# An output product built from seven block products: transformer block, forward and backward, on one core

## The chip, the cores and the metric

The kernel runs on one core of one Trainium2 chip. The metric is the time of one execution on the device, in microseconds. The core has a matrix engine (TensorE, PE in the profile), a vector engine (VectorE, DVE), a scalar engine (ScalarE, ACT), a general engine (GpSimd, POOL) and a queue engine (SyncE, SP). Matmuls read SBUF and write PSUM, the accumulator memory; the other engines read PSUM back. DMA engines move data between SBUF and HBM; SP, POOL and ACT issue their transfers.

## What is computed

One transformer block with linear attention and a SwiGLU feed-forward part, and its gradients: 2048 tokens, width 640, 32 heads of 20, feed-forward width 1728, all in bfloat16. The seven outputs are the block's result and the gradients of x, wqkv, wo, w_gate, w_up and w_down.

```python
def _A_ref(x, wqkv, wo):                      # linear attention
    pq, pk = phi(q), phi(k)                   # q, k, v from x @ wqkv
    kv = einsum("bhsd,bhse->bhde", pk, v); z = einsum("bhsd->bhd", pk)
    o = einsum("bhqd,bhde->bhqe", pq, kv) / (einsum("bhqd,bhd->bhq", pq, z)[..., None] + 1e-6)
    return o.reshape(B, S, D) @ wo
def _B_ref(x, w_gate, w_up, w_down):
    return (silu(x @ w_gate) * (x @ w_up)) @ w_down

h  = x + _A_ref(layernorm(x), wqkv, wo)
h2 = h + _B_ref(layernorm(h), w_gate, w_up, w_down)
out, grads = h2, vjp(grad_out)                # of x, wqkv, wo, w_gate, w_up, w_down
```

The change lies in the last product, h2 = h + m @ w_down, with m = silu(gate) * up.

## The kernel before

Tokens are cut into 16 tiles of 128. The width 640 is 5 blocks of 128, and a result row of 640 is computed as two chunks of 320 columns, each in its own PSUM bank. The feed-forward width 1728 is 13 blocks of 128 and a last one of 64.

The stages, in order: first layer norm, keys and queries; attention forward through folded weights; second layer norm; for each of four column groups of the feed-forward width, gate and up products, the elementwise part, and the weight gradients (`dw_group`, where dW_gate and dW_up are already made by seven block products with sums on VectorE); the backward pass through the feed-forward part into dh1; the gradients of the attention part (dk, dx, dW_q, dW_k); and last the output product. m was stored to HBM (`scr_m`) in the feed-forward stage, and h (`scr_h1`) in the attention stage.

The stage before the change, line 1024 on, walks over the tiles. For each it forms dk (`ps_dk`) and, three tiles later, dx (`ps_dxn`, 30 matmuls) with a layer norm backward (`ln_bwd`, lines 141 to 152): ACT reads PSUM, VectorE multiplies, ACT again, VectorE adds twice, and POOL stores dx. `dwqk(1, i)` is part i of dW_k: 32 matmuls that accumulate over the 16 token tiles, twice for the two chunks, then a convert on ACT (line 991) and a store. Parts 0 to 2 lie between the last tiles, parts 3 and 4 behind them.

The output stage takes one token tile after another (`part`, line 1121). A tile of m, transposed on load by SP (`load_mT`, line 1022), is the stationary operand, w_down (`wd`) the moving one. The 13 full blocks need 13 matmuls a chunk. The last block has only 64 rows: its matmul takes half of the array's rows. w_down's last 64 rows are held twice, in the lower and in the upper partitions, so that the half matmuls of two chunks can stand side by side on the two halves of the array. They are collected: `halves_at` does those of tiles 0 to 3 in one block of eight behind tile 1, of 4 to 7 behind tile 5, and so on, five blocks in all. VectorE adds h (`h1r`, loaded by POOL) to the finished PSUM row (line 1128), and POOL or SP stores it. Between tiles, `small_of` places the six blocks of dW_o (two matmuls each, line 1082) and the five of dW_v (seven small ones, line 127), each with a convert on ACT and a store. The operands of dW_v come from `scr_Yt` by six transposes on SP.

PSUM is four tiles of two banks (`mm`); a new one waits until an earlier one has been read. SBUF pools work in the same way: `big` has five large slots, `strips` four. In the region around this stage SP and DVE issue in the order in which the code is written; PE, ACT and POOL are ordered by the scheduler.

Of the kernel before, what the change touches and what calls it, by code (L numbers as in the profile page):

```python
# [8 lines left out]
FP32 = mybir.dt.float32  # L9
BF16 = mybir.dt.bfloat16  # L10
ALU = mybir.AluOpType
ACT = mybir.ActivationFunctionType
AX = mybir.AxisListType
EngineType = mybir.EngineType

P = 128
# [4 lines left out]
def kernel(  # L21
# [8 lines left out]
    nc = tc.nc  # L30
    _, S, D = A_x.shape
    F = B_w_gate.shape[1]
    Dh = D // H
    ST = S // P
    DT = D // P
    NCH = [(0, 320), (320, 640)]
    LAG = 3
# [6 lines left out]
    FT = 14  # L44
    GM = 448
    MTA = 5
# [5 lines left out]
    o0_v = out_0.rearrange("b (t p) d -> p (b t) d", p=P)  # L52
# [5 lines left out]
    big = ctx.enter_context(tc.tile_pool(name="big", bufs=5))  # L58
# [3 lines left out]
    def mm(name):  # L62

        return psum.tile([P, 2, 512], FP32, name=name, tag="mm")

    def row(ps):
        return ps[:, :, :320]

    def half(ap):
        return ap.rearrange("p (c n) -> p c n", c=2)  # L70
# [3 lines left out]
    def wk(name, w=D, pool=0):  # L74
        return wpools[pool].tile([P, w], BF16, name=name, tag="w", padded_shape=[P, D])
# [13 lines left out]
    scr_Yt = dram.tile([D, D], BF16, name="scr_Yt")  # L89
# [22 lines left out]
    OH = [120 * j for j in range(5)] + [D - P]  # L112
    HC = [(0, 120)] * 5 + [(88, P)]
    HG = len(OH)
# [64 lines left out]
    def fw(name):  # L179
        return fpool.tile([P, 2, GM], BF16, name=name, tag="f")  # L180
# [297 lines left out]
    with tc.manual_schedule(engines={EngineType.PE, EngineType.DVE, EngineType.SP, EngineType.Pool}):  # L478
# [25 lines left out]
        for i in range(DT):  # L504
            ps = mm("ps_y")
            for ci, (n0, n1) in enumerate(NCH):
                for t in range(ST):
                    nc.tensor.matmul(ps[:, ci, :320], lhsT=xn[:, t, i * P:(i + 1) * P], rhs=pk[:, t, n0:n1],  # L508
                                     start=(t == 0), stop=(t == ST - 1))
# [55 lines left out]
        for t in range(ST + 2):  # L565
            if t < ST:
                xr = wk("h1")
                ps = mm("ps_a")
                for ci, (n0, n1) in enumerate(NCH):
                    for i in range(DT):  # L570
                        nc.tensor.matmul(ps[:, ci, :320], lhsT=pqsT[:, i, t * P:(t + 1) * P], rhs=W2[:, i, n0:n1],  # L571
                                         start=(i == 0), stop=(i == DT - 1))
# [12 lines left out]
            while h1_todo and h1_todo[0][0] < t:  # L585
                v, h1 = h1_todo.pop(0)
# [5 lines left out]
            u = t - 2  # L592
# [23 lines left out]
    with tc.manual_schedule(engines={EngineType.SP}):  # L616
# [105 lines left out]
        for g in range(4):  # L722
            w = GW[g]
# [3 lines left out]
            for t in range(0, ST, 2):  # L727
                pg = mm("pg")
                for c in range(2):
                    for kt in range(DT):  # L730
                        nc.tensor.matmul(pg[:, c, :w], lhsT=hnT[:, kt, (t + c) * P:(t + c + 1) * P], rhs=wg[:, kt, 0:w],  # L731
                                         start=(kt == 0), stop=(kt == DT - 1))
                pu = mm("pu")
                for c in range(2):
                    for kt in range(DT):
                        nc.tensor.matmul(pu[:, c, :w], lhsT=hnT[:, kt, (t + c) * P:(t + c + 1) * P],  # L736
                                         rhs=wg[:, kt, w:2 * w], start=(kt == 0), stop=(kt == DT - 1))
                ddt = dd[t // 8]
                tt = t % 8
# [10 lines left out]
                u = fw("u")[:, :, :w]  # L750
# [88 lines left out]
    def mat(at, k, w):  # L839
        return mats[:, at:at + k * w].rearrange("p (k w) -> p k w", k=k)  # L840
# [5 lines left out]
    with tc.manual_schedule(engines={EngineType.SP, EngineType.Pool}):  # L846
# [20 lines left out]
        for t in range(ST + LAG_C):  # L867
# [14 lines left out]
            u = t - LAG_C + 1  # L882
# [15 lines left out]
            u = t - LAG_C  # L898
# [14 lines left out]
            S1 = small.tile([P, H], FP32, name="S1", tag="S1", bufs=3)  # L913
# [9 lines left out]
    with tc.manual_schedule(engines={EngineType.SP, EngineType.DVE}):  # L923
# [13 lines left out]
        def tr_cols(dst, src, c):  # L937
            nc.sync.dma_start_transpose(out=dst.unsqueeze(1), in_=src[:, c:c + P])
# [24 lines left out]
        Y = mat(2 * HG * P + HG * D, HG, D)  # L963
# [7 lines left out]
        def load_pqT(v):  # L971
            nc.sync.dma_start_transpose(out=ring[:, 4 + v % 3], in_=scr_pk[v * P:(v + 1) * P, :])
            nc.sync.dma_start_transpose(out=ring[:, 7 + v % 3], in_=dq[v // 8][:, v % 8, :])
# [4 lines left out]
            nc.scalar.copy(out=half(WK2[:, i, :]), in_=row(ps))  # L978
            nc.sync.dma_start_transpose(out=WV2[:, :, i * P:(i + 1) * P], in_=WK2[:, i, :])

        def dwqk(which, i, between=None):
            ev = wk("dwqk", pool=i % 2)
            ps = mm("ps_dwqk")
            for ci, (n0, n1) in enumerate(NCH):
                for t in range(ST):
                    nc.tensor.matmul(ps[:, ci, :320], lhsT=xn_r[:, t, i * P:(i + 1) * P],  # L986
                                     rhs=dq[t // 8][:, t % 8, n0:n1] if which == 0 else dk[:, t, n0:n1],
                                     start=(t == 0), stop=(t == ST - 1))
                if between and ci == 0:
                    between()  # L990
            nc.scalar.copy(out=half(ev[:]), in_=row(ps))
            nc.gpsimd.dma_start(out=out_2[i * P:(i + 1) * P, which * D:(which + 1) * D], in_=ev[:])

        load_pqT(0)
        for t in range(ST):
# [3 lines left out]
        for t in range(ZL, ZL + 2):  # L999
            dz_add(t, ztmp)  # L1000
        dwqk(0, 0)
        kv_blocks(dKVT, "ps_dkvt", lambda i, a, b: woT[:, i, a:b], lambda i, a, b: GT[:, i, a:b])
        for t in range(ZL + 2, ST):
            dz_add(t, ztmp)
        dzs = [wk("dzs"), wk("dzl")]
        nc.vector.tensor_copy(out=dzs[0][:], in_=zacc[:])
        nc.vector.tensor_tensor(out=dzs[1][:], in0=zacc[:], in1=dzs[0][:], op=ALU.subtract)
        dwqk(0, 1)
        for i in range(3):
            wk2(i)  # L1010
# [6 lines left out]
        mTs = {}  # L1017

        def load_mT(t):
            if t % 4 == 0:  # L1020
                mTs[t // 4] = strips.tile([P, 4, FT, P], BF16, name="mT", tag="S")
            nc.sync.dma_start_transpose(out=mTs[t // 4][:, t % 4], in_=scr_m[t * P:(t + 1) * P, :])

        for t in range(ST + LAG):
            if t in (2, 3):
                dwqk(0, t + 1)
            if t < ST:
                if t + 2 < ST:
# [7 lines left out]
                                               in1=half(dzb[:]), op0=ALU.mult, op1=ALU.add)  # L1036
# [11 lines left out]
            if t == ST:  # L1048
                wd = big.tile([P, FT, D], BF16, name="wd", tag="B")
# [3 lines left out]
            u = t - LAG  # L1053
# [6 lines left out]
            for ci, (n0, n1) in enumerate(NCH):  # L1060
                for k, (lhs, rhs) in enumerate(((dqT, wqkvT[:, 0:5]), (pkT, WV2), (dkT, wqkvT[:, 5:10]))):
                    for i in range(DT):
                        nc.tensor.matmul(ps[:, ci, :320], lhsT=lhs[:, i, :], rhs=rhs[:, i, n0:n1],  # L1063
                                         start=(k == 0 and i == 0), stop=(k == 2 and i == DT - 1))
# [5 lines left out]
            ln_bwd(ps, xn_r[:, u, :], rstd1[:, u:u + 1], dh1[:, u, :], dx[:], 0)  # L1070
            nc.gpsimd.dma_start(out=o1_v[:, u, :], in_=dx[:])

        for i in range(LAG, DT):
            dwqk(1, i)


        def dwo(j):
            h0, h1 = HC[j]
            ev = wk("dwo", pool=j % 2)
            ps = mm("ps_dwo")  # L1080
            for ci, (n0, n1) in enumerate(NCH):
                nc.tensor.matmul(ps[:, ci, :320], lhsT=KV[:, j, :], rhs=G[:, j, n0:n1], start=True, stop=True)
            nc.scalar.copy(out=half(ev[:]), in_=row(ps))
            nc.gpsimd.dma_start(out=out_3[OH[j] + h0:OH[j] + h1, :], in_=ev[h0:h1, :])
# [8 lines left out]
        h1rs = {}  # L1093

        def load_h1(t):
            h1rs[t] = wk("h1r", pool=t % 2)
            nc.gpsimd.dma_start(out=h1rs[t][:], in_=scr_h1_v[:, t, :])

        for t in range(3):
            load_h1(t)  # L1100
        small_of = {2: [(dwo, 0)], 3: [(dwo, 1)], 6: [(dwo, 2), (dwv, 0)], 7: [(dwo, 3), (dwv, 1)],
                    10: [(dwo, 4), (dwv, 2)], 11: [(dwo, 5), (dwv, 3)], 13: [(dwv, 4)]}
        halves_at = {1: range(4), 5: range(4, 8), 9: range(8, 12), 12: (12, 13), 14: (14, 15)}
        pso = {}

        def chunks(t):
            return NCH if t < ST - 1 else [(0, 320), (320, 512), (512, 640)]

        def po(t, ci):
            tile, bank = (0, ci) if t < ST - 1 else (ci % 2, ci // 2)  # L1110
            if (t, tile) not in pso:
                pso[t, tile] = mm("ps_o")
            n0, n1 = chunks(t)[ci]
            return pso[t, tile][:, bank, :n1 - n0]

        opened = set()

        def part(t, ci, j, h, last):
            n0, n1 = chunks(t)[ci]
            r = slice(0, P) if h is None else slice(64 * h, 64 * h + 64)  # L1120
            nc.tensor.matmul(po(t, ci), lhsT=mTs[t // 4][r, t % 4, j, :], rhs=wd[r, j, n0:n1],  # L1121
                             start=(t, ci) not in opened, stop=last)
            opened.add((t, ci))

        def finish(t):
            h1r = h1rs.pop(t)
            if t < ST - 1:
                nc.vector.tensor_tensor(out=half(h1r[:]), in0=row(pso.pop((t, 0))), in1=half(h1r[:]), op=ALU.add)  # L1128
                (nc.gpsimd if t < 10 else nc.sync).dma_start(out=o0_v[:, t, :], in_=h1r[:])
            return h1r  # L1130

        for t in range(ST):
            if t + MTA < ST:
                load_mT(t + MTA)
            if t < 3:
                for j in (2 * t, 2 * t + 1):
                    tr_cols(Y[:, j, :], scr_Yt, OH[j])
            if t + 3 < ST:
                load_h1(t + 3)
            if t == ST - 1:  # L1140
                h1r = finish(t)
            late = t in (0, 1, 4, 5, 8, 9, 12, 14)
            for ci, (n0, n1) in enumerate(chunks(t)):
                for j in range(FT - 1):
                    part(t, ci, j, None, j == FT - 2 and not late)
                if t == ST - 1:
                    nc.vector.tensor_tensor(out=h1r[:, n0:n1], in0=po(t, ci), in1=h1r[:, n0:n1], op=ALU.add)
                    (nc.sync, nc.scalar, nc.sync)[ci].dma_start(out=o0_v[:, t, n0:n1], in_=h1r[:, n0:n1])
            if t in halves_at:
                n = 0  # L1150
                for u in halves_at[t]:
                    for ci in range(len(chunks(u))):
                        part(u, ci, FT - 1, n % 2, u <= t)
                        n += 1
                for u in halves_at[t]:
                    if u <= t:
                        finish(u)
            elif not late and t < ST - 1:
                finish(t)
            for f, i in small_of.get(t, ()):  # L1160
                f(i)


# [28 lines left out]
```

## Time and profile before

| what | us |
|---|---|
| median of 3 runs | 801.68 (800.44 to 802.12) |
| the profiled execution | 800.75 |
| its span | 799.0 |
| PE busy | 793.6 |
| DVE busy | 536.6 |
| output stage, first to last matmul | 733 to 796 |

The span is cut into groups of instructions by line and shape. A row such as `ps_o<-wd,mT` names the tile written and the tiles read; the last columns are busy time, the mean length of one in ns, and how long the engine was idle just before, with what ended that. The chain of waits is followed back from the last instruction. A matmul's recorded length includes its way through the array (299 ns for 320 columns), while the next starts 136 ns later; the chain counts the latter.

### The profile page before, as it was taken

The page shows a single profiled execution, that of the slowest core. Times are in us where ns is not written, and L with a number is a line of the kernel's source. Part 1 is how long each engine was busy: PE and PEld are TensorE (multiplying, and loading weights), DVE is VectorE, ACT ScalarE, POOL GpSimd, SP SyncE. Part 2 cuts the span into 40 slices and gives each one's busy share as a digit, 9 for nine tenths or more (in the row PEclk, how much of TensorE's full clock was granted, in tenths as well). Part 3 has the DMA queues.
Part 4 walks back from the last instruction along what each step waited for, and adds up shares of the span by engine and source line. Part 5 has one row for each costly group of instructions (what it writes and reads, how often), then busy time and mean ns, then how long its engine had stood idle before and what let it go on. Part 6 is the DMA issues. An engine that isn't in the chain of part 4 may idle for free.

```text
span 799.0 us, 13637 instructions
## 1 busy us (share of the span) xinstructions
PE 793.6 (99%) x5357; PEld 510.9 (64%) x5357; DVE 536.6 (67%) x947; ACT 287.9 (36%) x414; POOL 172.9 (22%) x305
## 2 busy tenths in 40 slices
PE   9999999999999999999999999999999999999998
PEld 7776566555555555555665777777777777777676
DVE  7989988894497648744965169999897366621222
ACT  6962532760383145402821132233313133331010
POOL 4600047411201110012034011111301112112330
PEclk9999999999999999999999999999999999999999
DMA  9899999999679877892796667877598879899993
GB/s 259 161 240 308 195 215 271 273 268 232 139 175 227 221 165 195 227 224 71 166 259 176 245 150 201 204 198 173 127 217 183 154 147 171 165 252 235 203 220 104
DMA packets 286705, 160.12 MB, mean 200 GB/s; under 512 B 241564, under 2 KB 275485, under 8 KB 286640
## 3 DMA queue, kind: packets, MB, share of 16 engines
q1 hardware_dynamic: 268912, 99.56, 61.7%
q0 software_dynamic: 14832, 54.36, 22.5%
q10 hardware_dynamic: 2896, 5.33, 2.0%
q8 instruction: 42, 0.69, 0.4%
q14 instruction: 23, 0.19, 0.1%
HBM read 47.68 MB, written 53.66 MB: 127 GB/s over the span
## 4 chain that ended last, share of the span: by engine, by line
PE 89%; DMA 4%; DVE 3%; issue 1%; SPq 1%; POOL 0%; DVEq 0%; POOLq 0%
PE ps_dhn L108 15%; PE ps_dxn L1063 8%; PE ps_dw L806 8%; PE ps_o L1121 7%; PE pu L736 6%; PE ps_wa L646 6%; PE pg L731 6%; PE ps_dwqk L986 5%; PE ps_dm L417 5%; PE ps_kq L305 4%; PE ps_dk L108 3%; PE ps_y L508 3%; PE ps_gt L861 3%; PE ps_dp L108 3%; PE ps_a L571 3%; PE ps_wc L646 3%
## 5 line engine op out<-in xcount | busy, mean ns | idle before, releaser
L108 PE MATMUL ps_dhn<-wgT,cols 128*128 128x320 bf16 x864 | 119.5, 299 | 0.0
L108 PEld LDWEIGHTS <-cols 128*128 128x128 bf16 x864 | 84.5, 98 | 32.9
L146 DVE CUSTOM_DVE_ANT_0 lb_a<-lb_dy,hn 128x640 bf16<-128x640 bf16 x32 | 26.4, 825 | 59.0 <-ACT lb_dy L144 59.0
L731 PE MATMUL pg<-wgu,hnT 128*128 128x448 bf16 (+1 forms) x320 | 63.6, 346 | 0.0
L736 PE MATMUL pu<-wgu,hnT 128*128 128x448 bf16 (+1 forms) x320 | 63.6, 346 | 0.0
L1121 PE MATMUL ps_o<-wd,mT 128*128 128x320 bf16 (+3 forms) x462 | 61.1, 295 | 0.0
L806 PE MATMUL ps_dw<-m_s,dh 128*128 128x448 bf16 (+1 forms) x320 | 60.4, 346 | 0.0
L1063 PEld LDWEIGHTS <-ring 128*128 128x128 bf16 x480 | 47.0, 98 | 18.2
L1121 PEld LDWEIGHTS <-mT 128*128 128x128 bf16 (+1 forms) x462 | 41.8, 97 | 17.5 <-issue 2.6
L1063 PE MATMUL ps_dxn<-wqkvT,ring 128*128 128x320 bf16 x320 | 51.3, 299 | 0.0
L736 PEld LDWEIGHTS <-hnT 128*128 128x128 bf16 x320 | 31.3, 98 | 27.1
L806 PEld LDWEIGHTS <-dh 128*128 128x128 bf16 x320 | 31.3, 98 | 27.1
L731 PEld LDWEIGHTS <-hnT 128*128 128x128 bf16 x320 | 31.3, 98 | 27.0
L1128 DVE TENSOR_TENSOR h1r<-ps_o,h1r 128x640 bf16<-128x640 f32 x15 | 12.1, 822 | 52.6 <-PE ps_o L1121 49.3
L417 PEld LDWEIGHTS <-dh2T 128*128 128x128 bf16 x320 | 31.0, 98 | 25.1
L417 PE MATMUL ps_dm<-wdT,dh2T 128*128 128x448 bf16 (+1 forms) x240 | 46.5, 344 | 0.0
L144 ACT ACTIVATE lb_dy<-ps_dhn,rstd 128x640 bf16<-128x640 f32 x16 | 12.7, 794 | 91.3 <-PE ps_dhn L108 91.3
L305 PE MATMUL ps_kq<-wqk,xnT 128*128 128x320 bf16 x320 | 44.9, 299 | 0.8 <-DMA wqk<-in_A_wqkv_dram 0.4
L752 ACT ACTIVATE dd<-pg 128x896 bf16<-128x896 f32 (+1 forms) x32 | 28.5, 891 | 40.4 <-PE pg L731 38.0
L646 PEld LDWEIGHTS <-S 128*128 128x128 bf16 x256 | 25.0, 98 | 22.5 <-issue 0.9
L305 PEld LDWEIGHTS <-xnT 128*128 128x128 bf16 x320 | 30.9, 98 | 13.1 <-DMA xnT<-xn 0.7
L986 PEld LDWEIGHTS <-hn 128*128 128x128 bf16 x320 | 31.1, 98 | 11.9
(187 smaller groups left out, 1439.0 us busy)
## 6 DMA issues: line engine op xcount, KB each, us to landing
scr_dT<-stg SPq DMA_DIRECT2D x48, 224.0 KB, 2.9
cols<-scr_dT POOLq DMA_DIRECT2D x6, 1728.0 KB, 8.7
scr_m<-m_s POOLq DMA_DIRECT2D x12, 448.0 KB, 4.6
cols<-scr_dT ACTq DMA_DIRECT2D x2, 1728.0 KB, 10.7
scr_dT<-stg SPq DMA_DIRECT2D x16, 192.0 KB, 2.3
scr_pq<-pqa SPq DMA_DIRECT2D x4, 640.0 KB, 4.4
scr_xnT<-xnT SPq DMA_DIRECT2D x4, 640.0 KB, 5.2
scr_pk<-pk SPq DMA_DIRECT2D x4, 640.0 KB, 4.6
```

The costliest lines, as they stand in the source:

```text
L108: nc.tensor.matmul(ps[:, ci, :320], lhsT=lhs(k), rhs=rhs(k, *NCH[ci]), start=(start and k == 0), stop=(stop and k == n - 1))
L146: nc.vector.tensor_tensor_reduce(out=a[:], in0=dy[:], in1=xhat, scale=1.0, scalar=0.0, op0=ALU.mult, op1=ALU.add, accum_out=sums[:, 1:2])
L305: nc.tensor.matmul(ps[:, ci, :320], lhsT=xnT[:, t, k, :], rhs=wqk[:, k, w0 + n0:w0 + n1], start=(k == 0), stop=(k == DT - 1))
L417: nc.tensor.matmul(ps[:, c, :w], lhsT=dh2T[:, kt, (t + c) * P:(t + c + 1) * P], rhs=wdT[:, kt, o:o + w], start=(kt == 0), stop=(kt == DT - 1))
L646: nc.tensor.matmul(out, lhsT=lhs[:, t, :], rhs=rhs[:, t, :], start=(first and t == 0), stop=(t == 7), skip_group_check=not first)
L731: nc.tensor.matmul(pg[:, c, :w], lhsT=hnT[:, kt, (t + c) * P:(t + c + 1) * P], rhs=wg[:, kt, 0:w], start=(kt == 0), stop=(kt == DT - 1))
L736: nc.tensor.matmul(pu[:, c, :w], lhsT=hnT[:, kt, (t + c) * P:(t + c + 1) * P], rhs=wg[:, kt, w:2 * w], start=(kt == 0), stop=(kt == DT - 1))
L752: sig = nc.scalar.activation(out=dg, in_=pg[:, :, :w], func=ACT.Sigmoid)
L806: nc.tensor.matmul(ps[:, c, :w], lhsT=lhs(t), rhs=rhs(t), start=(t == 0), stop=(t == ST - 1))
L986: nc.tensor.matmul(ps[:, ci, :320], lhsT=xn_r[:, t, i * P:(i + 1) * P], rhs=dq[t // 8][:, t % 8, n0:n1] if which == 0 else dk[:, t, n0:n1] ...
L1063: nc.tensor.matmul(ps[:, ci, :320], lhsT=lhs[:, i, :], rhs=rhs[:, i, n0:n1], start=(k == 0 and i == 0), stop=(k == 2 and i == DT - 1))
L1121: nc.tensor.matmul(po(t, ci), lhsT=mTs[t // 4][r, t % 4, j, :], rhs=wd[r, j, n0:n1], start=(t, ci) not in opened, stop=last)
```

## The change

Tiles 0 to 13 are taken in seven pairs. A pair's m is cut into 2 x 2 blocks: upper and lower token tile, and w_down's blocks 0 to 5 and 6 to 11 (`HK = 6`). w_down is cut likewise, with its two column chunks. Where the plain way has eight products of six matmuls, Strassen's scheme (in Winograd's form) has seven, over sums of blocks: T1 to T4 from w_down, once, and S1 to S4 from m, for each pair. VectorE makes these sums in bfloat16 (`tt`), in two more tiles of the `big` pool (`ot`, `os`). Blocks 12 (full) and 13 (half) of the width are left over and are added directly (`left`), where T5, the difference of w_down's chunks in these blocks, corrects one corner.

The results run through PSUM bank A of the pair, to which product after product is added, and VectorE reads it in between: step a (products a11 B11 and a12 B21), b (S1 T1, into a bank of the tile `pcc` that all pairs share in turn), c (S2 T2), d (S3 T3), e (a22 T4), f (S4 B22). VectorE keeps the values in between in fp32 (`s1h`, `u2h`, `u3h`). Steps d, e and f of a pair are issued between the steps of the next pair. Each pair has seven evictions of 320 columns, and each half matmul of step a meets the one of the previous pair's step d; that of e meets that of f.

Tiles 14 and 15 stay as they were. dW_o's six blocks move between the quarters of dW_k's parts 3 and 4, and part 4's quarters fill the gaps of the first pair. dW_v's blocks follow pairs 3 to 6 and the tail. From here on PE and ACT also issue in the written order. Four tiles of h1 are loaded ahead instead of three, and the transposed loads of m stand before those of `scr_Yt`, two tiles for each pair.

```diff
-        def dwqk(which, i, between=None):
+        def dwqk_steps(which, i):
...
-                if between and ci == 0:
-                    between()
+                    if t == 7 or (t == ST - 1 and ci == 0):
+                        yield
             nc.scalar.copy(out=half(ev[:]), in_=row(ps))
             nc.gpsimd.dma_start(out=out_2[i * P:(i + 1) * P, which * D:(which + 1) * D], in_=ev[:])
+            yield
...
-        for i in range(LAG, DT):
-            dwqk(1, i)
...
+        def osum(p, i):
+            if p < NP:
+                S1, S2, S3, S4 = (os_v(p, k) for k in range(4))
+                a11, a12, a21, a22 = mblk(p, 0, 0), mblk(p, 0, 1), mblk(p, 1, 0), mblk(p, 1, 1)
+                (lambda: tt(S1, a21, a22, ALU.add), lambda: tt(S2, S1, a11), lambda: tt(S3, a11, a21),
+                 lambda: tt(S4, a12, S2))[i]()
...
+        def prod(out, lhs, rhs, start, stop):
+            for k in range(HK):
+                nc.tensor.matmul(out, lhsT=lhs[:, k, :], rhs=rhs[:, k, :], start=(start and k == 0),
+                                 stop=(stop and k == HK - 1), skip_group_check=not start)
+        def left(out, t, rhs, h, which=(0, 1)):
+            for w in which:
+                r = slice(64 * h, 64 * h + 64) if w else slice(0, P)
+                nc.tensor.matmul(out, lhsT=mTs[t // 4][r, t % 4, 12 + w, :], rhs=rhs[r, w, :], start=False,
+                                 stop=True, skip_group_check=True)
...
+        def step_a(p):
+            pa[p] = mm("ps_oa")
+            A, Dk, _ = bank(p)
+            prod(A, mblk(p, 0, 0), B11, True, True)
+            prod(Dk, mblk(p, 0, 1), B21, True, True)
+            left(Dk, 2 * p, BL[0], 0)
+            tt(s1h, A, h1v(2 * p, 0), ALU.add)
+            tt(h1v(2 * p, 0), Dk, s1h, ALU.add)
+        def step_b(p):
+            prod(bank(p)[2], os_v(p, 0), T1, True, True)
+        def step_c(p):
+            A = bank(p)[0]
+            prod(A, os_v(p, 1), T2, False, True)
+            tt(u2h[p % 2], A, h1v(2 * p, 1), ALU.add)
+        def step_d(p):
+            A = bank(p)[0]
+            left(A, 2 * p + 1, BL[1], 1, which=(1, 0))
+            prod(A, os_v(p, 2), T3, False, True)
+            tt(u3h, A, h1v(2 * p + 1, 1), ALU.add)
+        def c22(p):
+            tt(h1v(2 * p + 1, 1), bank(p)[2], u3h, ALU.add)
...
+        def step_e(p):
+            A = bank(p)[0]
+            prod(A, mblk(p, 1, 1), T4, False, True)
+            left(A, 2 * p + 1, T5, 0)
+            tt(h1v(2 * p + 1, 0), A, h1v(2 * p + 1, 0), ALU.add)
+            o_store(2 * p + 1)
+            pa.pop(p)
+        def step_f(p):
+            C = pcc[:, p % 2, :320]
+            left(C, 2 * p, BL[1], 1, which=(1, 0))
+            prod(C, os_v(p, 3), B22, False, True)
+            tt(h1v(2 * p, 1), C, u2h[p % 2], ALU.add)
+            o_store(2 * p)
+        with tc.manual_schedule(engines={EngineType.PE, EngineType.Activation}):
+            for t in range(4):
+                load_h1(t)
+            for t in (5, 6):
+                load_mT(t)
+            for j in range(2):
+                tr_cols(Y[:, j, :], scr_Yt, OH[j])
+            tt(T1, B12, B11)
+            osum(0, 0)
+            tt(T2, B22, T1)
+            osum(0, 1)
+            tt(T3, B22, B12)
+            osum(0, 2)
+            tt(T4, B21, T2)
+            tt(T5, BL[0], BL[1])
+            osum(0, 3)
+            fill = dwqk_steps(1, 3)
+            for j in range(4):
+                next(fill)
+                dwo(j)
+            fill = dwqk_steps(1, 4)
+            next(fill)
+            dwo(4)
+            pcc = mm("ps_oc")
+            for p in range(NP):
+                v = p - 1
...
+                step_a(p)
+                if v < 0:
+                    next(fill)
+                    osum(p + 1, 0)
+                    step_b(p)
+                    step_c(p)
+                    next(fill)
+                    osum(p + 1, 2)
+                    next(fill)
+                    osum(p + 1, 1)
+                    dwo(5)
+                    osum(p + 1, 3)
+                    continue
+                step_d(v)
+                step_b(p)
+                c22(v)
+                osum(p + 1, 0)
+                step_c(p)
+                step_e(v)
+                osum(p + 1, 2)
+                step_f(v)
+                osum(p + 1, 1)
+                osum(p + 1, 3)
+                if p >= 3:
+                    f, i = small_q.pop(0)
+                    f(i)
...
+            tail(ST - 2, 0, 320, p14[:, 0, :320])
+            step_d(v)
+            tail(ST - 2, 320, D, p14[:, 1, :320])
+            c22(v)
+            step_e(v)
+            step_f(v)
...
+            o_store(ST - 2)
+            for f, i in small_q:
+                f(i)
```

## The prediction

> **What bounds the kernel now.** I read the page's busy line, clock row and DMA row first, then the chain of waits from 724 us on, then the groups by shape, then what PE's weight loads wait for where half blocks occur, then SP's own queue in order of time.
>
> ```profile
> PE 793.6 (99%) x5357; PEld 510.9 (64%) x5357; DVE 536.6 (67%) x947; ACT 287.9 (36%) x414; POOL 172.9 (22%) x305
> PEclk9999999999999999999999999999999999999999
> DMA  9899999999679877892796667877598879899993
> ```
>
> PE is never idle and its granted clock never falls: a microsecond of matmuls taken away is a microsecond gained, unless a wait takes its place. DMA is busy too until the last slice.
>
> ```profile
> 724.52 8.69 PE ps_dwqk L986 x64
> 733.21 11.35 PE ps_o L1121 x86
> 744.57 0.27 PE ps_dwo L1082 x2
> 744.84 3.53 PE ps_o L1121 x26
> 760.26 0.29 PE ps_dwv L127 x7
> 780.67 7.55 PE ps_o L1121 x56
> 788.52 7.65 PE ps_o L1121 x69
> 796.20 0.29 DVE h1r L1147
> ```
>
> From 724.52 to 796.17 the chain is PE alone. 26 full matmuls take 3.53 us: 0.136 each. The piece of 86 is 78 full ones (10.59) and 8 half-height ones (0.76); the piece of 56 is 52 full (7.06) and 4 halves (0.49). Four more halves, two pairs, cost 0.27, so a pair side by side costs one full matmul (0.135). The rest, 0.22 in both pieces, is a fixed price for each block of halves, whatever its length: going into the half-height form and out again.
>
> ```profile
> 740.21 0.39 PEld L1121 LDWEIGHTS <-mT 64*128 64x128 bf16 x8 [0.26 <-issue]
> 740.86 1.20 PEld L1121 LDWEIGHTS <-mT 128*128 128x128 bf16 x10 [0.26 <-issue]
> ```
>
> The weight loads stop at exactly these two places, into the halves and out of them. The kernel pays that five times.
>
> ```profile
> L642 DVE TENSOR_TENSOR dd<-dd 128x3584 bf16<-128x3584 bf16 x9 | 17.9, 2021 | 16.8 <-PE ps_wa L646 16.8
> L642 DVE TENSOR_TENSOR S<-hn 128x1024 bf16<-128x1024 bf16 x16 | 9.9, 683 | 0.0
> L764 DVE TENSOR_TENSOR nsg<-nsg,dd 128x768 bf16<-128x768 bf16 x8 | 4.4, 550 | 0.0
> L1147 DVE TENSOR_TENSOR h1r<-ps_o,h1r 128x320 bf16<-128x320 f32 x1 | 0.5, 492 | 1.3 <-PE ps_o L1121 1.3
> 205.68 1.29 DVE L642 TENSOR_TENSOR S<-hn,S 128x1024 bf16<-128x1024 bf16 x2
> 728.03 0.49 DVE L152 TENSOR_TENSOR dx<-lb_a,dh 128x640 bf16<-128x640 bf16 x1
> ```
>
> These price the sums: DVE work now sparse after 728. Two S sums of 0.68 take 1.29, so one follows the other 0.08 before its recorded end.
>
> ```profile
> 742.26 2.15 SPq L1022 DMA_TRANSPOSE mT<-scr_m  x1
> 744.46 5.98 SPq L1022 DMA_TRANSPOSE mT<-scr_m  x1
> 750.48 4.09 SPq L1022 DMA_TRANSPOSE mT<-scr_m  x1
> 754.61 4.07 SPq L1022 DMA_TRANSPOSE mT<-scr_m  x1
> ```
>
> Four loads of m (tokens 8 to 11) hold SP for 16.4 us, 4.1 each; PE spends 3.8 on a tile (two tiles from 744.84 to 752, with small work). The loads of m run only some 10 us ahead of PE.
>
> **PE's matmuls.** A pair of tiles now costs 2 x 2 x 13 = 52 full matmuls and two pairs of halves. After: seven products of 6, four full leftovers, two pairs of halves: 46. Seven pairs save 42 full matmuls, 42 x 0.136 = **-5.71**. Tiles 14 and 15, dW_o, dW_v and dW_k keep their counts.
>
> **The halves.** Today they stand in 5 blocks. After, the leftover of the product b21 (end of step a) meets that of step d, and e's meets f's: two blocks in each of the iterations 1 to 6, one alone in pair 0's step a, one alone in the tail's step d, one e/f block in the tail, and the last block of five halves: 16. Eleven more at 0.22, less 0.01 as the last form lies closer to 0.21: **+2.3**. Two halves now have no partner, one slot more: **+0.14**. PE's sum: **-3.3**. This holds a rule against the change: the Trainium skill, TensorEngine Tiling (Array Packing), Key Properties, says that changing the tiling mode drains the TensorE, and gives no price; TensorE: Matmul & The Clock Gate, step 4 of Part 2, gives a drain of about 128 cycles, from which I estimate 0.05 us a switch, 22 more switches 1.2 us and a PE sum of -4.4. The rows show 0.22 a block, and the row decides.
>
> **VectorE's sums before pair 0.** DVE, SP, PE and ACT issue in the written order here, so the nine first sums stand behind the last layer norm of dx (728.03) and ahead of pair 0's evictions. T1 to T4 have 6 x 320 = 1920 elements: between the 1024 and 3584 rows that is 0.683 + 896 x 0.522 ns = 1.15 each; four S sums of 768 at 0.55; T5 (640) 0.49. By durations 7.3, with 0.08 overlap at each 6.6. So S4 is through at 735.1 to 735.9 and the eviction s1 of A (0.49) at 735.6 to 736.4. PE: 724.52 + dW_k part 3 (4.35) + four dW_o blocks (1.09) + a quarter part (1.09) + dW_o (0.27) = 731.3; step a 13 full, a lone half and its switch 2.1: 733.4; second quarter 734.5; step b 735.3. Step c writes into A, so it waits for s1: 0.3 to 1.1. A convert of dW_o on ACT can also come ahead of the layer norm's (ready at 726.5) and shift everything by 0.3. I take **+0.5**, near the overlapped end since back-to-back rows show overlap; bounds 0 and 2. The top also takes in pair 0's h1 load landing late: POOL issues it at 729.35 now, behind the dx store, and it lands 4.4 us later at 733.8, but two stores of dW_o are now ready for POOL at about the same time, 0.55 each. h1 is read in that same s1, with the later sums queued behind it in DVE.
>
> **The PSUM tile of pair 1.** Four two-bank tiles exist; in iteration 0 they are pair 0's, the shared C tile, dW_k's part 4 and dW_o's. Pair 1's step a needs the one that ACT empties after dW_k's last quarter. Today that convert ends 0.89 after PE's next work begins (733.05 to 733.94, 0.69 of it the convert), and only dW_o's last block (0.27) lies between: **+0.6**, bounds 0 and 0.8. In the tail, the last dW_v block needs the C tile, free only after f's eviction (0.30 matmul latency, 0.04, 0.49), with some 0.6 of PE work ahead of it: **+0.2**, bounds 0 and 0.5.
>
> **Steady iterations.** DVE has four S (0.55) and seven evictions of 320 columns (0.49): 5.6 by durations, against 46 x 0.136 + 2 pairs x 0.135 + 2 x 0.22 = 6.97 us of PE. Laid out in order, counting from the iteration's start: u3 is ready at 3.8 and step e wants it at 4.7; c22 is through at 4.3 and f wants C at 5.7; the last S sum ends 1.7 into the next iteration, where s1 follows at 2.1 and step c wants it at 3.9. I cost the sums at nothing; the cover is that 0.9 us, and past it each iteration would lose what DVE is late. The sums of fp32 and bf16 halves read PSUM as the L1147 row does. In the four groups of dW_gate and dW_up, which are built of the same seven products, PE waited for such a sum once, 0.7 us.
>
> **Loads and queues.** Bytes do not change. POOL issues four h1 loads instead of three at the start, then two per pair, two pairs ahead: 14 us against landings of at most 9.9, so nothing. The six dW_o blocks move ahead of pair 1, each with two matmuls (counted), a convert on ACT (0.69) and a store on POOL (0.55): their operands landed before 700, and after the start of the stage, costed above, they hide under PE. SP loses its stop for dW_v's first store ahead of tokens 12 to 14. For m, starting from SP's 726.75, eight loads at 4.1 and six transposes of scr_Yt (9.3 together) have token tile 13 issued at 768.9 and landed, 5 to 7 later, at 773.5 to 776. Pairs 1 to 6 start at 739.7, 746.7, 753.6, then with a dW_v block each 760.9, 768.1 and 775.4. S1 of pair 6 stands 4.1 into pair 5's iteration, at 772.2, and stops PE only when DVE then keeps back u2, which the next step d needs, some 3.5 later, at 776. **0**, bounds 0 and +4: no gain is possible since PE waits for no load now. The end, tile 15's three chunks, last add and store, is unchanged.
>
> **Sum.** -5.71 + 2.3 + 0.14 + 0.5 + 0.6 + 0.2 = **-2.0 us**. The profiled execution took 800.75 (span 799.0), 0.1% under the median of 801.68; against the median this gives **799.7**.
>
> **The rivals.** (1) *Start later than laid out, or DVE late by 0.2 in each iteration*: for it, the strict order and only 0.9 us of cover; against it, the row-by-row order above. Another 1.5 us: 801.2, no change. (2) *m comes too late, slower*: the S sums want both tiles of a pair before PE does, at the head of DVE's queue. For it, 4.1 us a load and 5.98 for one; against it, later ones took 2.1. At 4.1 it just fits; at 5 a load, eight loads put tile 13 at 781 and cost 5: 804.5 or so. It decides (slower by 1.6) when tile 13 lands after 779.5. (3) *No stops at the start*, because s1 and the tile come free earlier: PE's -3.3 alone, 798.4. (4) *The half switches cost no more than today*, hidden under other waits: -5.7 + 0.6 = -5.1 at most, 796.5; the 0.22 in two pieces and two stopped weight loads speak against it. That the seven products don't cut matmuls is excluded by the code.
>
> **How the numbers follow.** Forecast 0.48, (1) 0.22, (2) 0.14, (3) 0.10, (4) 0.06. A measurement of this kernel tells about 0.2%, 1.6 us, from no change: faster is below 800.1, slower above 803.3. The forecast's own range, 798.9 to 800.7, lies four fifths below 800.1: 0.38, with (3) and (4) 0.54; same takes the remaining 0.10 and most of (1): 0.30; slower 0.16. The range 797.8 to 803.2 leaves out (4) and most of (2), under 0.2.
>
> **What would show it.** 420 matmuls with wd or a T as moving operand in place of 462; 16 pairs of stopped weight loads at 0.26; one PE wait for DVE's s1 near 735 and one for ACT's dW_k convert near 740; PE else unbroken; its last matmul near 794. PE waits on S sums that in turn wait for an mT transpose, from pair 4 on, would make it wrong on the slow side; half blocks under 0.1 on the fast side.

## The result

The changed kernel takes 802.57 us (median of 20 executions), the kernel before 802.62 (20). The ratio of the means, 802.39 to 803.35 without the changed kernel's one slow execution of 811.77, is 0.9988, with a 95% interval of 0.9969 to 1.0007. That can't be told from no change: 1 us less, give or take 1.5. The forecast was 2.0 us less, at 799.7; it started from a median of 801.68 for the kernel before, which itself comes out 0.9 higher here. The profile tells more than the total does, because much of the scatter comes from a place outside the change.

The page of the changed kernel: the span, the engines' busy time, and the clock row.

```profile
span 803.4 us, 13640 instructions
PE 792.6 (99%) x5315; PEld 506.5 (63%) x5315; DVE 566.8 (71%) x1015; ACT 287.8 (36%) x414; POOL 172.6 (21%) x305
PEclk9999999999999999999998999999999999999999
```

PE has 5315 matmuls, 42 fewer than the 5357 before. The span is nevertheless 4.4 us longer than the profiled one of before, and the clock row has one slice below full. So this execution lost something. The next view says where. It is the output stage alone, from the end of the last dx matmul to the end of the last matmul, in the changed kernel (the columns after the stretch are the busy time and count of PE, PEld, DVE, ACT and POOL, then the granted clock, the DMA share and GB/s):

```profile
730.35:800.55 70.20, 68.75 (x531) 46.25 (x529) 45.31 (x90) 10.39 (x16) 17.25 (x32) 1.00 0.88 194
```

and the same stage in the kernel before:

```profile
724.52:796.17 71.65, 71.64 (x573) 50.83 (x571) 14.92 (x22) 10.41 (x16) 19.00 (x35) 1.00 0.92 193
```

The stage became 1.45 us shorter, with 30 us more work on VectorE, but it began 5.8 us later. The chain of waits shows what came before it, in code that the change doesn't touch, the last group of the feed-forward gradients. First the kernel before:

```profile
434.70 0.97 DVE dwev L642
435.71 2.76 PE ps_wc L646 x16
```

then the changed kernel:

```profile
434.75 0.53 POOL pkr L933
435.29 0.47 POOL out_dram L810
435.82 2.16 DMA out_dram<-dwev
438.10 0.97 DVE dwev L642
439.11 5.18 PE ps_wc L646 x16
```

An eviction on VectorE waits for a store, and PE waits for the eviction: 0.9 us in the profile of before, 4.6 in this one (from start to start of the matmuls, less the 0.16 us that one of 384 columns takes; between the recorded end and the next start PE's timeline has 0.69 and 4.44), after which 16 matmuls took 5.18 us in place of 2.76. The granted clock averaged 0.72 from 435 to 447 us, against 1.00 in the kernel before. (The Trainium skill, TensorE: Matmul & The Clock Gate, Part 1, says that the clock falls to half when PE has been idle for a window of about 3.4 us; a stop of 4.6 that halves the pace and one of 0.9 that doesn't agree with it.) Two of the runs below lie in between: after a stop of 2.96 us (more blocks) the 16 matmuls took the same 2.76, after one of 3.39 (one eviction moved) 4.11. The stop has another length in each profile, and the two experiments on POOL's queue below take it away: the executions then lie within 1.4 and 1.6 us, where twelve of the kernel before in the same session lie within 3.4. That all of the scatter above comes from it is not shown. What points to it is the clock: the nine executions of the changed kernel with a mean granted clock of 1.000 took 799.4 to 802.7 us, the eleven with less 802.3 to 811.8, and in the profile of one of these the clock is below full only here.

Inside the stage, the chain of the changed kernel around the places that the prediction named:

```profile
726.26 4.09 PE ps_dxn L1069 x30
...
740.41 0.47 DVE os L1123
740.88 0.41 DVE ot L1123
741.30 0.02 issue
741.32 0.50 DVE h1r L1123
741.82 0.04 issue
741.86 0.97 PE ps_oa L1139 x6
742.84 2.19 PE ps_dwqk L986 x16
745.03 0.03 ACTq L991
745.05 0.04 issue
745.09 0.70 ACT dwqk L991
745.79 0.04 issue
745.84 1.79 PE ps_oa L1139 x12
747.63 0.62 PE ps_oa L1146 x4
...
751.51 0.38 PE ps_oa L1146 x2
751.88 0.25 PE ps_oc L1146 x2
...
795.97 0.50 DVE h1r L1123
796.47 0.04 issue
796.51 0.45 PE ps_dwv L127 x7
796.96 3.58 PE ps_o L1268 x39
```

Three stops are to be seen. Pair 0's step c (741.86) waits for VectorE, whose nine first sums and two evictions run until then. Pair 1's step a (745.84) waits for ACT's convert of dW_k's part 4. The last dW_v block (796.51) waits for the eviction of the C tile. From the starts of the matmuls they are 0.88, 0.72 and 0.31 us. Everywhere else PE is unbroken. A meeting of two half matmuls with a full one on each side is the pieces of `L1146`, the line of `left`: 0.62 us for what is three slots of 0.136 (a slot is the time from one matmul's start to the next), so 0.21 for the switches. The weight loads stop there each time:

```profile
751.57 0.34 PEld L1146 LDWEIGHTS <-mT 64*128 64x128 bf16 x3 [0.26 <-issue]
754.64 0.34 PEld L1146 LDWEIGHTS <-mT 64*128 64x128 bf16 x3 [0.27 <-issue]
```

### The profile page after: what moved, and what is told of

Read it like the earlier page. It is cut to its first block, busy times and chain, and to the rows that moved or that the text cites. A ratio compares the mean times of both kernels' runs of the same rounds, so it can differ in the third digit from the quotient of the medians.

```text
span 803.4 us, 13640 instructions
## 1 busy us (share of the span) xinstructions
PE 792.6 (99%) x5315; PEld 506.5 (63%) x5315; DVE 566.8 (71%) x1015; ACT 287.8 (36%) x414; POOL 172.6 (21%) x305
## 4 chain that ended last, share of the span: by engine, by line
PE 87%; DVE 4%; DMA 4%; issue 2%; SPq 1%; POOL 0%; ACT 0%; DVEq 0%; POOLq 0%; ACTq 0%
PE ps_dhn L108 15%; PE ps_dxn L1069 8%; PE ps_dw L806 8%; PE ps_wa L646 6%; PE pu L736 6%; PE pg L731 6%; PE ps_dm L417 5%; PE ps_dwqk L986 5%; PE ps_kq L305 4%; PE ps_oa L1139 3%; PE ps_wc L646 3%; PE ps_dp L108 3%; PE ps_y L508 3%; PE ps_gt L861 3%; PE ps_dk L108 3%; PE ps_a L571 3%
## 5 line engine op out<-in xcount | busy, mean ns | idle before, releaser
L772 POOL DMA_DIRECT2D scr_m<-m_s x16 | 12.1, 756 | 122.6 <-DVE m_s L764 122.6
L642 DVE TENSOR_TENSOR dd<-dd 128x3584 bf16<-128x3584 bf16 (+1 forms) x12 | 23.1, 1953 | 21.2 <-PE ps_wa L646 21.2
L150 ACT ACTIVATE lb_a<-hn,lb_k 128x640 bf16<-128x640 bf16 x32 | 29.5, 920 | 21.7 <-DVE lb_k L149 18.8
```

The costliest lines, as they stand in the source:

```text
L150: nc.scalar.activation(out=a[:], in_=xhat, func=ACT.Identity, scale=k[:, 1:2], bias=k[:, 0:1])
```

## The experiments

The theory: PE bounds the stage, the seven products take 5.7 us away, the eleven more blocks of halves give 2.2 back, the two halves without a partner 0.14, and the three stops another 1.9. Rivals: VectorE is late as a whole, so that the stops would only move; the switches cost nothing by themselves; the transposed loads bound the stage. For each run the stage is the time from the last dx matmul to the end of the last matmul, as in the two rows above; it doesn't contain the stop near 436 us.

**Full-height leftovers.** If switches cost what the rows say, it pays to do without them, though more matmuls are needed.

```diff
-                for r in (0, 64):
-                    nc.sync.dma_start(out=wd[r:r + 64, 13, :], in_=B_w_down[13 * P:F, :])
+                nc.vector.memset(wd[64:P, 13, :], 0.0)
+                nc.sync.dma_start(out=wd[0:64, 13, :], in_=B_w_down[13 * P:F, :])
...
-                r = slice(64 * h, 64 * h + 64) if w else slice(0, P)
-                nc.tensor.matmul(out, lhsT=mTs[t // 4][r, t % 4, 12 + w, :], rhs=rhs[r, w, :], start=False,
+                nc.tensor.matmul(out, lhsT=mTs[t // 4][:, t % 4, 12 + w, :], rhs=rhs[:, w, :], start=False,
...
```

> Changed kernel with the lower copy of w_down's last 64 rows set to zero and every half-height matmul made full-height, so there is no half-height form in the stage. Theory (a block of halves costs 0.20 us for the two switches): 16 blocks gone, -3.2; 33 single full matmuls in place of 18 slots, +2.0; the stage goes from 70.20 to 69.0, and no weight load stops for 0.26 any more. Rival (the switches are hidden, or the rows read them wrongly): the extra matmuls alone, 72.2.

The stage took 69.0 us, 1.2 less, as expected. In its chain the same two meetings read:

```profile
742.43 0.54 PE ps_oa L1145 x4
...
746.23 0.27 PE ps_oa L1145 x2
746.50 0.27 PE ps_oc L1145 x2
```

Four matmuls now take 0.54 us, four slots of 0.136, where two full and two halves side by side took 0.62. So a pair of halves that is alone is dearer than two full matmuls, half of whose rows multiply zeros.

**More blocks in the kernel before.** The same price, without any of Strassen's products.

```diff
-        halves_at = {1: range(4), 5: range(4, 8), 9: range(8, 12), 12: (12, 13), 14: (14, 15)}
+        halves_at = {**{t: (t,) for t in range(14)}, 14: (14, 15)}
...
-            late = t in (0, 1, 4, 5, 8, 9, 12, 14)
+            late = t < ST - 1
```

> Kernel before, with each tile's two half-height matmuls issued directly behind the tile instead of collected: 15 blocks in place of 5, nothing else. Theory: 10 more blocks at 0.20, so the stage goes from 71.65 to 73.65 us. Rival (switches hidden): 71.65.

The stage went from 71.65 to 73.8 us: 2.1 for ten more blocks, 0.21 each. The weight loads of the halves stood still for 4.0 us in 15 blocks, 0.26 each:

```profile
L1121 PEld LDWEIGHTS <-mT 64*128 64x128 bf16 x33 | 1.5, 93 | 4.0 <-issue 4.0
```

The matmul count is the same, so this is the switch alone. Together with the full-height run, the rival of hidden switches is out.

**VectorE's sums twice.** The four sums of pairs 1 to 6 are each issued two times.

```diff
-                (lambda: tt(S1, a21, a22, ALU.add), lambda: tt(S2, S1, a11), lambda: tt(S3, a11, a21),
-                 lambda: tt(S4, a12, S2))[i]()
+                for _ in range(2 if p else 1):
+                    (lambda: tt(S1, a21, a22, ALU.add), lambda: tt(S2, S1, a11), lambda: tt(S3, a11, a21),
+                     lambda: tt(S4, a12, S2))[i]()
```

> Changed kernel with the four S sums of pairs 1 to 6 each made twice, 1.9 us more on VectorE in each of six iterations. Theory (sums lie under PE with about 0.9 us of cover where step c wants s1, and VectorE has some 1.5 to 2 us idle in an iteration): at most 0.5 us per iteration shows, the stage stays between 70.2 and 73. Rival (VectorE is already late in each iteration, no cover): all of it shows, 81 us.

The stage took 72.0 us, 1.8 more, for 11.7 us more work on VectorE. Five iterations showed new stops ahead of step c, of 0.43, 0.59, 0.29, 0.30 and 0.24 us. The cover can be read from VectorE's timeline in the changed kernel, where it is idle 1.43 us in each iteration, always until PE is done:

```profile
754.98 0.49 DVE L1123 TENSOR_TENSOR ot<-ps_oa,h1r 128x320 f32<-128x320 f32 x1 [0.46 <-PE ps_oa L1146]
756.86 0.49 DVE L1123 TENSOR_TENSOR h1r<-ps_oc,ot 128x320 bf16<-128x320 f32 x1 [0.32 <-PE ps_oc L1139]
758.87 0.49 DVE L1123 TENSOR_TENSOR h1r<-ps_oa,h1r 128x320 bf16<-128x320 f32 x1 [0.65 <-PE ps_oa L1146]
```

So the sums as they are cost nothing; the rival that VectorE is late in each iteration is out; with twice the sums it would have been near the mark, 1.8 us against the 1.5 that the prediction gave it.

**The order of pair 0.** Both remaining quarters of dW_k's part 4 come between steps b and c.

```diff
                     step_b(p)
-                    step_c(p)
                     next(fill)
                     osum(p + 1, 2)
                     next(fill)
+                    step_c(p)
                     osum(p + 1, 1)
```

> Changed kernel with pair 0's order altered: both remaining quarters of dW_k's part 4 come between steps b and c, so that step c no longer stands where PE waited 0.88 us for VectorE's s1, and ACT's convert of that part runs beside step c, so that pair 1 no longer waits 0.72 us for its PSUM tile. Theory (PE is the bound, the two waits are local and nothing is late behind them): the stage, from the last dx matmul to the last matmul, goes from 70.20 to 68.6 us. Rival (VectorE is late as a whole, the stops only move): PE waits the same 1.6 us at a later step, 70.2.

The stops of 0.88 and 0.72 us were both gone, and the stage took 69.1 us, 1.1 less instead of 1.6. A new stop of 0.47 us came at the first dW_v block, which the chain leads back to SP's queue:

```profile
753.28 1.56 SPq L1028
754.84 0.04 issue
754.88 1.85 SPq L938
756.73 0.04 issue
756.77 4.28 DMA mats<-scr_Yt
761.05 0.05 issue
761.10 0.19 PE ps_dwv L127
```

The last transposes of `scr_Yt` (L938) stand behind the loads of m (L1028) and land just before 761.1, 35.4 us after the last dx matmul. In the profile of the changed kernel the last one landed after 31.5 us, 5 us ahead of its use, so that PE would have found it there even coming 1.6 us sooner, as in this run. Here three loads of m in a row held SP for 6.5, 4.8 and 4.1 us, there for 3.3, 2.6 and 4.2; the edit doesn't touch them, and why they differ is not shown. So the rival of loads that come late was not true of the m tiles, but in this execution it was true of dW_v's operands, whose landing the prediction had not timed.

**One eviction moved.** PE began step c 0.56 us after s1, which the prediction says it waits for, but 0.04 after the next eviction, which reads the tile's other bank.

```diff
-            tt(h1v(2 * p, 0), Dk, s1h, ALU.add)
+            if p:
+                tt(h1v(2 * p, 0), Dk, s1h, ALU.add)
...
                     step_c(p)
+                    tt(h1v(0, 0), bank(0)[1], s1h, ALU.add)
                     next(fill)
```

> Changed kernel with one VectorE instruction of pair 0 moved: the second eviction of step a, which reads the tile's other bank, is issued behind step c's eviction instead of ahead of step c. Theory (in the changed kernel step c waited for both evictions of the two-bank tile, since PE started 0.04 us after the second one's end and 0.56 after s1's): PE's wait before step c falls from 0.88 to about 0.37 us and the stage from 70.20 to 69.7. Rival (step c waits for s1 alone, or for the sums S2 and T2, and the nearness to the second eviction is chance): the wait stays at 0.88.

The stop before step c fell from 0.88 to 0.36 us. Now step c follows s1 (`ot`) directly:

```profile
739.17 0.41 DVE ot L1123
739.58 0.04 issue
739.62 0.97 PE ps_oa L1139 x6
```

So in the changed kernel step c waited for the evictions of both banks, though it writes only one. (That a tile of two banks is guarded as a whole is inferred: the tile is all that step c and the second eviction share.) The stage as a whole took 70.4 us in place of the expected 69.7, because dW_v's first block now waited 0.69 us, at the place and for the transposes that the run before showed. The last of them landed 36.7 us after the last dx matmul.

**POOL's queue near 436 us, in both kernels.** Three loads for a later loop stood in POOL's queue, each waiting for a staging buffer, ahead of the feed-forward stage's last stores. The first two are now issued later, and the third follows them.

```diff
...
-        load_pk(0)
-        load_pk(1)
+        with tc.issue_after(last_out6):
+            load_pk(0)
+            load_pk(1)
```

Here `last_out6` is the last store of dW_down. On the changed kernel:

> Changed kernel with POOL's first loads of phi(k) for the dk loop issued only behind the last store of dW_down, so that they no longer stand, waiting for a staging buffer, ahead of the feed-forward stage's last weight-gradient stores. Theory (the spread between executions comes largely from PE's stop near 436 us, 0.9 to 4.7 us so far, because those stores and the eviction behind them wait on POOL's queue): the stop shrinks below 0.5 us in the profile and the time is 2 to 3 us shorter. Rival (the stop has another cause, the transposed feed-forward stores themselves): it stays between 0.9 and 4.7 and the time stays.

On the kernel before:

> Kernel before with the same shift of POOL's first loads. Theory: the stop near 436 us is gone here too, about 2 us shorter than the kernel before. Against the changed kernel with the same shift it then shows the output stage's own difference without that noise: 1.4 us longer. Rival: the time is that of the kernel before.

The stop is gone in both: the 16 matmuls follow the ones before without a gap, here in the changed kernel with this shift:

```profile
426.76 7.80 PE ps_wa L646 x48
434.56 2.60 PE ps_wc L646 x16
```

The changed kernel then takes 798.41 us (797.97 to 799.39, 5 executions), a ratio to the kernel before of 0.9956 (0.9942 to 0.9970); the kernel before with the shift 799.60 (799.26 to 800.83, 8), 0.9975 (0.9964 to 0.9985). All eight profiles without the shift show the stop, 0.9 to 4.6 us long, and none of the three with it. With it out of the way the two kernels differ by 1.2 us, and by 1.4 in the spans of their profiles (796.3 and 797.7): what the stage says.

**Fewer blocks, and no stops.** The halves of e and f of one pair and of a and d of the next are put into one block at the end of each iteration; dW_k's quarters are moved as above, with the last one behind step c; dW_v goes where a PSUM tile is free and its operands have landed.

```diff
-        def left(out, t, rhs, h, which=(0, 1)):
...
+        def left(out, t, rhs, w, h=0):
+            r = slice(64 * h, 64 * h + 64) if w else slice(0, P)
+            nc.tensor.matmul(out, lhsT=mTs[t // 4][r, t % 4, 12 + w, :], rhs=rhs[r, w, :], start=False,
+                             stop=True, skip_group_check=True)
...
+        def halves_e(v):
+            left(bank(v)[0], 2 * v + 1, T5, 1, 0)
+            left(bank(v)[2], 2 * v, BL[1], 1, 1)
+
+        def halves_a(p):
+            left(bank(p)[1], 2 * p, BL[0], 1, 0)
+            left(bank(p)[0], 2 * p + 1, BL[1], 1, 1)
...
                 step_f(v)
                 osum(p + 1, 1)
+                halves_e(v)
+                halves_a(p)
+                finish_e(v)
+                finish_a(p)
                 osum(p + 1, 3)
-                if p >= 3:
-                    f, i = small_q.pop(0)
-                    f(i)
...
```

> Changed kernel with one block of half-height matmuls for each pair instead of two (those of e and f of the pair before with those of a and d of this one, at the end of the iteration), the quarters of dW_k between b and c of pair 0, and dW_v's last two blocks in the tail where a PSUM tile is free. Theory: 8 blocks fewer at 0.20 and one slot less, -1.7; the three waits of 0.88, 0.72 and 0.31 go but for some 0.3: the stage goes from 70.20 to about 66.9 us. Rival (something else is late by then, VectorE behind the evictions that now come together, or the transposed loads): above 68.5.

The stage took 66.9 us, 3.3 less than in the changed kernel, as expected. Its chain, in which the one stop that is left, 0.48 us at pair 1, is for the same convert on ACT, and an iteration's four halves take 0.38 us, with one switch going in:

```profile
738.14 0.70 ACT dwqk L991
738.84 0.04 issue
738.88 1.79 PE ps_oa L1139 x12
...
745.29 0.24 PE ps_oa L1144
745.53 0.00 PE ps_oc L1144
745.53 0.14 PE ps_oa L1144 x2
```

With POOL's loads shifted as well:

> The merged version with POOL's first loads shifted as well. Theory: 3.3 us in the stage and about 2 near 436 us under the changed kernel, 4.7 in the stage under the kernel before: about 796 us. Rival (waits move): 799 or more.

It takes 795.03 us (794.53 to 795.54, 4 executions); the ratio to the kernel before is 0.9911 (0.9897 to 0.9924). It beats both kernels: its longest execution is 3.8 us below the shortest of the changed kernel. Of the 6.9 us, 4.7 are the stage and the rest the stop near 436 us.

## Why the prediction was right or wrong

*Matmuls taken away, -5.71.* Right: 42 fewer, and the slots around the switches keep 0.136 us.

*Blocks of halves, +2.3, and the lone halves, +0.14.* Right. The stage's 1.45 us and the three stops' 1.91 together make PE's own sum -3.36, where -3.3 was forecast. Two experiments give 0.20 and 0.21 for a block. The estimate from a drain of 128 cycles (the Trainium skill, TensorE: Matmul & The Clock Gate, Part 2), half of that, would have made the gain 1.0 too large. The rule that a change of mode drains the array (the Trainium skill, TensorEngine Tiling (Array Packing), Key Properties) agrees with the pauses here; their price is 0.10 us each way.

*Step c of pair 0 waits for s1, +0.5.* This is the step that failed, though within its bounds: step c waits for more than s1. The sums ran as laid out: s1 ended 10.95 us after the last dx matmul, where 11.1 to 11.9 was worked out. But step c waited for the next eviction too, because it writes into a tile whose other bank that one still reads: 0.88. The moved eviction shows the wait: for s1 alone it was 0.36, a little less than the 0.5 forecast, and the second eviction added 0.52. h1's load was no part of it.

*Pair 1's PSUM tile, +0.6, and dW_v in the tail, +0.2.* Right in kind, 0.72 and 0.31; each was sized by 0.1 too little.

*Steady iterations, 0.* Right: no stop in any, and doubled sums cost 1.8 us of 11.7.

*Loads, 0.* Right for the changed kernel, and for m with more room than the text says: eight loads held SP for 22.0 us and not 33, and token tile 13 landed 39.2 us after the last dx matmul, where 49 to 51.5 was worked out. What comes late first is not m but dW_v's transposed operands, and that changes from one execution to the next: 31.5 us after the last dx matmul in the changed kernel, 35.4 and 36.7 in the two runs that stopped for them.

*The total.* -2.0 was forecast against the stage's -1.45; the stops were 0.6 larger. Measured over whole executions it is -1.0, within -2.5 and +0.6, and the likeliest case was faster by over 0.2%, where the measurement can't tell it from no change. That 802.57 lies within 797.8 and 803.2 says little for the working: that range is 5.4 us wide, and the forecast is 2.9 away. What bears the working out is the stage, and the two kernels without the stop near 436 us, which differ by 1.2. What the prediction left out is that an unrelated stop near 436 us changes by several microseconds from one execution to the next; the profile of before showed it, as a wait of 0.7 us, and the text even cites it, as a wait for a sum and a sign that such chains run smoothly, where it was an eviction that waited for a store.

## What to carry to other kernels

Count a rearrangement's changes of matmul form as well as its matmuls: here 2.2 of the 5.7 us that the seven products saved went into eleven more short blocks of half-height matmuls, at 0.2 us each, and collecting them won most of that back, padding them to full height about half. Where a stage is bound by PE without a gap, lay out the first and last rounds instruction by instruction: each stop was there, none in the steady state. And when whole executions scatter by more than the change is worth, compare the stage in the profile, and look for the wait that differs between two profiles in code that nobody touched.

## What the runs showed of the hardware

- A change between full-height and half-height matmuls costs PE 0.10 us each way, the weight loads pausing 0.26; two half-height matmuls on the two halves of the rows cost one full slot (0.135).
- A transposed load of m held SP for 4.1 us on average in the kernel before (16.4 us for four, at a DMA share of 1.11) and for 2.8 in the changed one (22.0 for eight, at 1.19). In two of the runs a transposed load that stood behind others on SP's queue became the next thing that PE waited for.
- After a stop of 4.6 us PE worked at half pace for 16 matmuls (0.32 us each for 384 columns in place of 0.16), at a granted clock of 0.50 from 438 to 444 us; after stops of up to 2.96 us it kept its pace.
- A load on POOL's queue that waited for its buffer held back the stores behind it, and through them PE, for 0.9 to 4.6 us in eight profiles and not at all in the three in which the loads were issued later.
